# Weights loaded ahead of q and k, conversion steps at even places, and the weights' low parts made by VectorE

## The chip, the cores and the metric

The kernel runs as one program on one core of a Trainium2 chip. TensorE (PE) multiplies, VectorE (DVE), ScalarE (ACT) and GpSimd (POOL) do the elementwise work, and the queue of SyncE (SP) issues all transfers between HBM and the core's memory. The metric is device microseconds of one execution.

## What is computed

Chunked attention on 8 x 8 heads (chunks of 64 tokens), then a gated network with an RMS norm, then a second network. All is float32, on 4608 rows of 512.

```python
def _attn_ref(q, k, v):                       # 8 batches, 8 heads, 576 tokens, 64 wide; chunks of 64
    ...
    scores = scale * np.matmul(q_c, k_c.transpose(0, 1, 2, 4, 3))
    scores = scores - np.max(scores, axis=-1, keepdims=True)
    attn = np.exp(scores)
    attn = attn / (np.sum(attn, axis=-1, keepdims=True) + 1e-09)
    out = np.matmul(attn, v_c)
    ...
def _moe_ref(x, w_gate, w_val, w_out, rms_g): # 512 -> 1536 -> 512
    rms = np.sqrt(np.mean(x * x, axis=-1, keepdims=True) + 1e-06)
    xn = x / rms * rms_g
    g = xn @ w_gate
    silu = g * (1.0 / (1.0 + np.exp(-g)))
    val = xn @ w_val
    return (silu * val @ w_out).astype(np.float32)
    ...
def _moe2_ref(x, w_in, w_out):                # 512 -> 2048 -> 512
    h = x @ w_in
    relu6 = np.clip(h + 3.0, 0.0, 6.0)
    g = h * relu6 / 6.0
    return (g @ w_out).astype(np.float32)
```

## The kernel before

The rows are worked in nine blocks of 512. The first network passes over blocks 0 to 8 and leaves its result in HBM; the second passes over them again. Every number that goes into a large matmul is split into a high part in the reduced format float32r and a low part, the rest, so that a product is three matmuls (high x high, low weight x high, high weight x low).

**Weight pieces.** The weights come in pieces of 512 KB, stored as 64-bit numbers: 36 in the first network, in the order gate, val, out for each f of 0 to 11, and 32 in the second. `Prep.load` (L121) issues the load of the next piece on SP. A piece then passes four stages, two pieces (a pair) at a time: `mag` (ScalarE, L138), `bits` (VectorE, L145, L147, L149, L153, each once per piece), which makes a float32 of the 64-bit number, `hi` (ScalarE, L160), and `lo`, the low part (GpSimd, L168: piece minus high part). `Prep.step(n)` advances the pipeline by one: `lo` of the pair of three steps ago, `hi`, `bits`, and `mag` of a new pair. Raw pieces and converted ones share a pool of 36 buffers; `held` counts them, and `Prep.fill(slots, most=4)` loads while `held + 3 <= slots`, at most `most` pieces a call. The last two pieces lie in a pool of their own.

**Start.** Before block 0 the lists LOADS and START, written by hand, interleave the loads of 16 pieces, the attention of the first four groups of 128 rows, and the stages of the first pieces. After it come q, k (`load_qk`, 64 small transfers on SP, L391) and v (`load_v`, 16 transfers, L401) of pair 4. A pair is 256 rows of attention; pairs 4 and 5 are the input of block 1.

**Block 0.** For each f: gate's matmuls (`mm_up`, 12 of L542), ScalarE's sigmoid (L688), VectorE's product (L689); val's matmuls, a second product on VectorE (L694), the split of the result (ScalarE L580 for `ah`, GpSimd L581 for `al`); then the 12 matmuls of the previous f's `out` (L551 to L554). After each of these three groups stands a hook, numbered hk = 3f + o, with o = 0, 1, 2. `att_hook` does one of a pair's attention steps there, a pair in five f: o = 1 of the first f turns q and k (VectorE, L405, L406) and issues the next pair's q and k; o = 0 of the second does the scores on PE (L418), o = 1 maximum, difference and exponent; the third sum and division (L446 to L454), the fourth the transposes, the fifth the values, squares (L501) and the issue of the next v. The step `rms` of the next block stands at the first f after two pairs. `prep_hook` calls `prep_a.step(HKA[hk])` where HKA is not 0, and `fill` after it. The gate and val results have one bank of PSUM each, so gate's matmuls of f + 1 wait for the product L689 of f.

**What sets the order.** Each engine executes its instructions in program order. The program's order is that of the Python code (a manual schedule), and a wait for another engine or a transfer holds all that stands behind it on the same engine. SP waits, at each transfer, for its eighth predecessor to land, and for the buffer to be free: the q and k loads of a pair reuse the buffers that L405 and L406 of the pair before have read.

In the second network the pieces are converted in the last block of the first (HKB at its hooks) and in the first block of the second; `lo` is the same function there.

Of the kernel before, what the change touches and what calls it, by code (L numbers as in the profile page):

```python
# [36 lines left out]
    square3 mean2 spread1 norm1 spread0 root2 squares3 mean3 wl2 inv2 root3 wh3 hi1 spread2 norm0 inv3 wm5  # L37
    norm2 hi2 lo1 spread3 hi0 lo2 norm3 hi3 lo3 wh4 wm6 lo0 wl3 wb5 wb6 wh5 wl4
""".split()
HKA = [2, 0, 0, 0, 2, 2, 0, 2, 0, 0, 2, 0, 2, 0, 2, 0, 0, 2, 2, 2, 0, 0, 2, 2, 2, 2, 2, 2, 0, 0, 2, 0, 0, 2, 0, 2]  # L40
HKB = [2, 2, 2, 2, 2, 2, 0, 2, 0, 2, 2, 0, 2, 0, 2, 0, 0, 2, 2, 2, 0, 2, 0, 2, 0, 0, 2, 2, 0, 2, 2, 2, 0, 0, 0, 0]


# [1 line left out]
def fused_kernel(  # L45
# [13 lines left out]
    nc = tc.nc  # L59
# [44 lines left out]
    class Prep:  # L104
# [59 lines left out]
        def lo(self, ids):  # L164
            for i in ids:
                w = W[self.pieces[i]]
                self.held -= not self.own(i)
                nc.gpsimd.tensor_tensor(  # L168
                    w[:, 1, :], self.raw.pop(i)[:, :, 0].bitcast(F32), w[:, 0, :].bitcast(F32), op=ALU.subtract
                )  # L170

# [340 lines left out]
    def rms(blk):  # L512

        ps = PS[:, ATT, :]
        nc.tensor.matmul(ps, ones, sqs.pop(blk), start=True, stop=True)
        rt = at_p.tile([128, N], F32, tag="kT", name="rt")
        nc.scalar.activation(rt, ps, AF.Sqrt, scale=1.0 / DM, bias=eps)
        nc.vector.reciprocal(rt, rt)
        x = xf[blk]
        for c in range(KD):  # L520
            nc.vector.scalar_tensor_tensor(
                out=x[:, c, :], in0=x[:, c, :], scalar=g_sb[:, c:c + 1], in1=rt, op0=ALU.mult, op1=ALU.mult
            )
# [53 lines left out]
    def split_act(t):  # L577
        hi = ah_p.tile([128, N], F32R, tag="ah", name="ah")
        lo = al_p.tile([128, N], F32R, tag="al", name="al")
        nc.scalar.copy(hi, t)  # L580
        nc.gpsimd.tensor_tensor(lo, t, hi.bitcast(F32), op=ALU.subtract)  # L581
        return hi, lo
# [30 lines left out]
    with tc.manual_schedule():  # L613
# [3 lines left out]
        prep_a, prep_b = Prep(a_pieces), Prep(b_pieces)  # L617
# [15 lines left out]
        sqs.pop(0)  # L633
        xf.pop(0)

        nxt = Pair(N // TP)
        nxt.load_qk()
        nxt.load_v()
        state = {"att": nxt}

        def att_hook(b, hk):

            if b + 1 >= NB:
                return
            f, o = divmod(hk, 3)
            t, g = divmod(f, 5)
            a = state["att"]
            if t == N // TP:
                if hk == 3 * f + 1 and g == 0:
                    rms(b + 1)  # L650
                return
            if (g, o) == (0, 1):
                a.run("turn")
                if a.i + 1 < NPR:
                    state["nxt"] = Pair(a.i + 1)
                    state["nxt"].load_qk()
            elif (g, o) == (1, 0):
                a.run("scores")
            elif (g, o) == (1, 1):
                a.run("top", "less", "expo")  # L660
            elif (g, o) == (2, 1):
                a.run("total", "share")
            elif (g, o) == (3, 1):
                a.run("trans_p", "out_p")
            elif (g, o) == (4, 1):
                a.run("values", "out_x", "square", "squares")
                if "nxt" in state:
                    state["att"] = state.pop("nxt")
                    state["att"].load_v()

        def prep_hook(b, hk):
            if b == 0 and not prep_a.done() and HKA[hk]:
                prep_a.step(HKA[hk])
                prep_a.fill(36)
            if b == NB - 1:
                if HKB[hk]:
                    prep_b.step(HKB[hk])
                prep_b.fill(hk)

        for b in range(NB):  # L680
            prev = None
            hk = 0
            if b == NB - 1:
                load_x2(0)
            for f in range(FA):
                mm_up(GB, W["gate", f], xs)
                s = sg_p.tile([128, N], F32, tag="sg", name="sg")
                nc.scalar.activation(s, PS[:, GB, :], AF.Sigmoid)  # L688
                nc.vector.tensor_tensor(s, s, PS[:, GB, :], op=ALU.mult)  # L689
                att_hook(b, hk)  # L690
                prep_hook(b, hk)
                hk += 1
                mm_up(VB, W["val", f], xs)
                nc.vector.tensor_tensor(s, s, PS[:, VB, :], op=ALU.mult)  # L694
                a = split_act(s)
                att_hook(b, hk)
                prep_hook(b, hk)
                hk += 1
                if prev is not None:
                    mm_down_a(W["out", f - 1], prev, f == 1, False)  # L700
                att_hook(b, hk)
                prep_hook(b, hk)
                hk += 1
                prev = a
# [7 lines left out]
        for b in range(NB):  # L712
# [3 lines left out]
            for f in range(FB):  # L716
# [10 lines left out]
                a = split_act(s)  # L727
# [36 lines left out]
```

## Time and profile before

| | us |
|---|---|
| median of 3 runs | 1869.09 (1868.18 to 1870.5) |
| profiled execution | 1870.38 |
| its span, first to last instruction | 1868.6 |
| PE busy | 1782.3 (95%), 9856 matmuls |
| VectorE, ScalarE, GpSimd busy | 727.0, 601.1, 542.4 |
| first matmul of block 0 / of block 1 | 54.33 / 212.19 |
| end of the chain, by engine | PE 82%, VectorE 6%, SP's queue 3%, GpSimd 2%, transfers 2% |

Engine names in rows: PE matmul, PEld weight load, DVE VectorE, ACT ScalarE, POOL GpSimd, SPq the queue of SyncE. "a<-b" is output and input by the program's tile names: `wraw` a loaded piece, `wtmp` a scratch tile of its conversion, `w` a converted piece, `sg` the activations, `XH` and `XL` the block's input. Shares over the whole span hide that block 0 of the first network and the conversions of the second have limits of their own; rows below are therefore taken by stretch.

### The profile page before, as it was taken

The numbers are of one execution on the slowest core, as the hardware profiler recorded it, in microseconds if no ns is written. First come the engines' busy times: TensorE is split into PE (matmuls) and PEld (weight loads), VectorE is DVE, ScalarE is ACT, GpSimd is POOL, SyncE is SP. The second block draws the span as 40 slices with busy tenths as digits, with TensorE's granted clock in tenths as the row PEclk, the third lists the DMA queues.
The fourth block names the chain that finished last, engine by engine and source line by source line (L and its number), as shares of the span: only waits on it lengthen the run. The fifth ranks groups of instructions, "written<-read, shape, count | busy, mean of one in ns | idle before, by whom it ended". The sixth has DMA issues, their size and how long they took to land.

```text
span 1868.6 us, 24155 instructions
## 1 busy us (share of the span) xinstructions
PE 1782.3 (95%) x9856; PEld 1457.4 (78%) x9856; DVE 727.0 (39%) x930; ACT 601.1 (32%) x899; POOL 542.4 (29%) x395
## 2 busy tenths in 40 slices
PE   5678999999999999999999889999999999999999
PEld 4556788888888888888887678888888888888887
DVE  7787534344353534335359951121212121212121
ACT  5344423233232323233234432222323232322222
POOL 3534322112121212112125652222223232323222
PEclk8789999999999999999999999999999999999999
DMA  9362211212212121212034410110101010101000
GB/s 249 78 170 70 49 31 44 41 28 49 40 40 45 39 44 26 51 36 46 12 102 153 142 55 1 46 36 10 46 0 46 1 46 1 45 1 46 0 23 23
DMA packets 225199, 93.88 MB, mean 50 GB/s; under 512 B 192960, under 2 KB 213440, under 8 KB 223936
## 3 DMA queue, kind: packets, MB, share of 16 engines
q1 hardware_dynamic: 225088, 92.34, 18.8%
q8 instruction: 77, 1.26, 0.3%
q14 instruction: 34, 0.28, 0.1%
HBM read 73.40 MB, written 18.87 MB: 49 GB/s over the span
## 4 chain that ended last, share of the span: by engine, by line
PE 82%; DVE 6%; SPq 3%; issue 3%; POOL 2%; DMA 2%; ACT 1%; DVEq 0%; POOLq 0%; ACTq 0%
PE PS L542 45%; PE PS L563 7%; PE PS L559 7%; PE PS L560 7%; PE PS L551 4%; PE PS L552 4%; PE PS L554 4%; SPq L391 2%; POOL w L168 2%; DVE wtmp L149 1%; DVE wraw L153 1%; PE PS L418 1%; DMA wraw<-in_moe_w_gate_dram 1%; PE PS L478 1%; DVE wtmp L145 1%
## 5 line engine op out<-in xcount | busy, mean ns | idle before, releaser
L542 PE MATMUL PS<-XH,w 128*128 128x512 f32 x2880 | 729.6, 396 | 41.8 <-DVE sg L689 29.4
L581 POOL TENSOR_TENSOR al<-sg,ah 128x512 fp32r<-128x512 f32 x252 | 334.0, 1325 | 1279.9 <-ACT ah L580 1279.9
L542 PEld LDWEIGHTS PS<-XH,w 128*128 128x128 f32 x2880 | 547.5, 191 | 163.9 <-DVE sg L689 33.7
L542 PE MATMUL PS<-XL,w 128*128 128x512 f32 x1440 | 389.0, 392 | 0.0
L724 DVE SCALAR_TENSOR_TENSOR sg<-sg,PS 128x512 f32<-128x512 f32 x144 | 99.2, 689 | 623.5 <-ACT sg L723 623.5
L542 PEld LDWEIGHTS PS<-XL,w 128*128 128x128 f32 x1440 | 273.8, 190 | 57.7
L580 ACT CAST ah<-sg 128x512 fp32r<-128x512 f32 x252 | 156.3, 620 | 429.6 <-DVE sg L694 313.9
L723 ACT ACTIVATE sg<-PS,three 128x512 f32<-128x512 f32 x144 | 99.1, 688 | 445.8 <-PE PS L542 431.5
L559 PE MATMUL PS<-w,ah 128*128 128x512 f32 x576 | 224.5, 390 | 2.8 <-ACT ah L580 2.8
L560 PE MATMUL PS<-w,ah 128*128 128x512 f32 x576 | 224.1, 389 | 0.0
L689 DVE TENSOR_TENSOR sg<-sg,PS 128x512 f32<-128x512 f32 x108 | 74.0, 685 | 274.7 <-ACT sg L688 274.6
L551 PE MATMUL PS<-ah,w 128*128 128x512 f32 x432 | 175.8, 407 | 0.2 <-ACT ah L580 0.2
L552 PE MATMUL PS<-ah,w 128*128 128x512 f32 x432 | 168.5, 390 | 0.0
L563 PE MATMUL PS<-w,al 128*128 128x512 f32 x576 | 154.9, 390 | 2.1 <-POOL al L581 2.1
L688 ACT ACTIVATE sg<-PS 128x512 f32<-128x512 f32 x108 | 64.4, 596 | 246.1 <-PE PS L542 229.5
L559 PEld LDWEIGHTS PS<-w,ah 128*128 128x128 f32 x576 | 108.1, 188 | 26.4 <-ACT ah L580 4.0
L563 PEld LDWEIGHTS PS<-w,al 128*128 128x128 f32 x576 | 108.2, 188 | 25.2 <-POOL al L581 2.9
L560 PEld LDWEIGHTS PS<-w,ah 128*128 128x128 f32 x576 | 108.2, 188 | 22.4
L694 DVE TENSOR_TENSOR sg<-sg,PS 128x512 f32<-128x512 f32 x108 | 74.2, 687 | 120.5 <-PE PS L542 117.1
L554 PE MATMUL PS<-al,w 128*128 128x512 f32 x432 | 115.8, 390 | 0.1
L168 POOL TENSOR_TENSOR w<-wraw,w 128x512 fp32r<-128x512 f32 x68 | 102.0, 1525 | 17.9 <-ACT w L160 17.9
L551 PEld LDWEIGHTS PS<-ah,w 128*128 128x128 f32 x432 | 81.1, 188 | 21.4 <-ACT ah L580 2.8
(85 smaller groups left out, 1229.0 us busy)
## 6 DMA issues: line engine op xcount, KB each, us to landing
wraw<-in_moe_w_out_dram SPq DMA_DIRECT2D x28, 512.0 KB, 5.2
yd<-yst SPq DMA_DIRECT2D x18, 512.0 KB, 3.4
xf<-yd SPq DMA_DIRECT2D x9, 1024.0 KB, 6.5
wraw<-in_moe_w_in_dram SPq DMA_DIRECT2D x16, 512.0 KB, 3.9
out_dram<-ost SPq DMA_DIRECT2D x16, 512.0 KB, 3.2
wraw<-in_moe_w_gate_dram SPq DMA_DIRECT2D x12, 512.0 KB, 6.5
wraw<-in_moe_w_val_dram SPq DMA_DIRECT2D x12, 512.0 KB, 7.4
v<-in_v_dram SPq DMA_DIRECT2D x96, 64.0 KB, 2.6
```

The costliest lines, as they stand in the source:

```text
L168: nc.gpsimd.tensor_tensor(w[:, 1, :], self.raw.pop(i)[:, :, 0].bitcast(F32), w[:, 0, :].bitcast(F32), op=ALU.subtract)
L542: nc.tensor.matmul(ps, w[:, wi, c * 128:(c + 1) * 128], xs[c][xi], start=(i == 0), stop=(i == n - 1))
L551: nc.tensor.matmul(ps, wm[0], a[0], start=first, stop=False)
L552: nc.tensor.matmul(ps, wm[1], a[0], start=False, stop=False)
L554: nc.tensor.matmul(PS[:, YB + m, :], w[:, 0, m * 128:(m + 1) * 128], a[1], start=False, stop=last)
L559: nc.tensor.matmul(PS[:, YB + m, :], am, w[:, 0, :], start=first, stop=False)
L560: nc.tensor.matmul(PS[:, YB + m, :], am, w[:, 1, :], start=False, stop=False)
L563: nc.tensor.matmul(PS[:, YB + m, :], a[1][:, m * 128:(m + 1) * 128], w[:, 0, :], start=False, stop=last)
L580: nc.scalar.copy(hi, t)
L581: nc.gpsimd.tensor_tensor(lo, t, hi.bitcast(F32), op=ALU.subtract)
L723: nc.scalar.activation(s, PS[:, bank, :], AF.Relu, bias=three)
L724: nc.vector.scalar_tensor_tensor(out=s, in0=s, scalar=6.0, in1=PS[:, bank, :], op0=ALU.min, op1=ALU.mult)
```

## The change

Four things change. HKA becomes a step of two pieces at every even hook. After the start, `prep_a.fill(36, 36)` loads as many pieces as the buffers hold (16 more) ahead of q and k of pair 4, v of pair 4 is issued at hook 0, and `fill` runs at every hook of block 0 until the pieces are done. The attention steps of block 0 stand one f (three hooks) later, and so does `rms`. The low part L168 is computed by VectorE instead of GpSimd, in the start, in block 0 and in the second network's conversions.

```diff
--- before.py
+++ after.py
@@ -37,7 +37,7 @@
     square3 mean2 spread1 norm1 spread0 root2 squares3 mean3 wl2 inv2 root3 wh3 hi1 spread2 norm0 inv3 wm5
     norm2 hi2 lo1 spread3 hi0 lo2 norm3 hi3 lo3 wh4 wm6 lo0 wl3 wb5 wb6 wh5 wl4
 """.split()
-HKA = [2, 0, 0, 0, 2, 2, 0, 2, 0, 0, 2, 0, 2, 0, 2, 0, 0, 2, 2, 2, 0, 0, 2, 2, 2, 2, 2, 2, 0, 0, 2, 0, 0, 2, 0, 2]
+HKA = [0 if hk % 2 else 2 for hk in range(36)]
 HKB = [2, 2, 2, 2, 2, 2, 0, 2, 0, 2, 2, 0, 2, 0, 2, 0, 0, 2, 2, 2, 0, 2, 0, 2, 0, 0, 2, 2, 0, 2, 2, 2, 0, 0, 0, 0]
 
 
@@ -165,7 +165,7 @@
             for i in ids:
                 w = W[self.pieces[i]]
                 self.held -= not self.own(i)
-                nc.gpsimd.tensor_tensor(
+                nc.vector.tensor_tensor(
                     w[:, 1, :], self.raw.pop(i)[:, :, 0].bitcast(F32), w[:, 0, :].bitcast(F32), op=ALU.subtract
                 )
 
@@ -633,9 +633,9 @@
         sqs.pop(0)
         xf.pop(0)
 
+        prep_a.fill(36, 36)
         nxt = Pair(N // TP)
         nxt.load_qk()
-        nxt.load_v()
         state = {"att": nxt}
 
         def att_hook(b, hk):
@@ -643,10 +643,17 @@
             if b + 1 >= NB:
                 return
             f, o = divmod(hk, 3)
+            a = state["att"]
+            if b == 0:
+                if hk == 0:
+                    a.load_v()
+                    return
+                f -= 1
             t, g = divmod(f, 5)
-            a = state["att"]
+            if t < 0:
+                return
             if t == N // TP:
-                if hk == 3 * f + 1 and g == 0:
+                if o == 1 and g == 0:
                     rms(b + 1)
                 return
             if (g, o) == (0, 1):
@@ -669,8 +676,9 @@
                     state["att"].load_v()
 
         def prep_hook(b, hk):
-            if b == 0 and not prep_a.done() and HKA[hk]:
-                prep_a.step(HKA[hk])
+            if b == 0 and not prep_a.done():
+                if HKA[hk]:
+                    prep_a.step(HKA[hk])
                 prep_a.fill(36)
             if b == NB - 1:
                 if HKB[hk]:
```

On SP, behind the last load of the start, stood in the kernel before (L391 and L401 are q, k and v of pair 4, L131 weight pieces):

```order
L131 DMA wraw<-in_moe_w_gate_dram 128x4x256
L391 DMA q<-in_q_dram 32x2x32 x16
L391 DMA q<-in_q_dram 32x6x32 x16
L391 DMA k<-in_k_dram 32x2x32 x16
L391 DMA k<-in_k_dram 32x6x32 x16
L401 DMA v<-in_v_dram 64x64 x8
L401 DMA v<-in_v_dram 64x3x64 x8
L131 DMA wraw<-in_moe_w_val_dram 128x4x256
L131 DMA wraw<-in_moe_w_out_dram 128x1024
L131 DMA wraw<-in_moe_w_gate_dram 128x4x256
```

and stand in the changed kernel, after fourteen more pieces behind the last one of the start, the fifteenth and sixteenth and what follows them:

```order
L131 DMA wraw<-in_moe_w_gate_dram 128x4x256
L131 DMA wraw<-in_moe_w_val_dram 128x4x256
L391 DMA q<-in_q_dram 32x2x32 x16
L391 DMA q<-in_q_dram 32x6x32 x16
L391 DMA k<-in_k_dram 32x2x32 x16
L391 DMA k<-in_k_dram 32x6x32 x16
L401 DMA v<-in_v_dram 64x64 x8
L401 DMA v<-in_v_dram 64x3x64 x8
L391 DMA q<-in_q_dram 32x8x32 x16
L391 DMA k<-in_k_dram 32x8x32 x16
```

Sixteen pieces have moved ahead of the 64 transfers of q and k. Further down, where pair 6's q and k and the last four pieces stand, SP's order is the same in both kernels:

```order
L401 DMA v<-in_v_dram 64x4x64 x8
L391 DMA q<-in_q_dram 32x4x32 x32
L391 DMA k<-in_k_dram 32x4x32 x32
L131 DMA wraw<-in_moe_w_out_dram 128x1024
L131 DMA wraw<-in_moe_w_gate_dram 128x4x256
L131 DMA wraw<-in_moe_w_val_dram 128x4x256
L131 DMA wraw<-in_moe_w_out_dram 128x1024
```

There nothing moved on SP; the loads L391 wait for the transposes L405 and L406 of pair 5, and those stand three hooks later. On VectorE, from the products of f = 0 on, stood before (L689 and L694 are the two products of an f):

```order
L689 TENSOR_TENSOR sg<-sg,PS 128x512
L694 TENSOR_TENSOR sg<-sg,PS 128x512
L405 STREAM_TRANSPOSE qT<-q 128x1024
L406 STREAM_TRANSPOSE kT<-k 128x1024
L689 TENSOR_TENSOR sg<-sg,PS 128x512
L694 TENSOR_TENSOR sg<-sg,PS 128x512
L428 TENSOR_REDUCE mx<-PS 128x16
L438 TENSOR_TENSOR p<-PS,mx 128x2x4x64 x2
L145 TENSOR_SCALAR wtmp<-wtmp 128x512 x2
L147 TENSOR_SCALAR wtmp<-wtmp 128x512 x2
```

and now (the same two products are L697 and L702):

```order
L697 TENSOR_TENSOR sg<-sg,PS 128x512
L702 TENSOR_TENSOR sg<-sg,PS 128x512
L168 TENSOR_TENSOR w<-wraw,w 128x512 x2
L145 TENSOR_SCALAR wtmp<-wtmp 128x512 x2
L147 TENSOR_SCALAR wtmp<-wtmp 128x512 x2
L149 SCALAR_TENSOR_TENSOR wtmp<-wraw,wtmp 128x512 x2
L153 SCALAR_TENSOR_TENSOR wraw<-wraw,wtmp 128x512 x2
L697 TENSOR_TENSOR sg<-sg,PS 128x512
L702 TENSOR_TENSOR sg<-sg,PS 128x512
L405 STREAM_TRANSPOSE qT<-q 128x1024
L406 STREAM_TRANSPOSE kT<-k 128x1024
L168 TENSOR_TENSOR w<-wraw,w 128x512 x2
```

The transposes of pair 4 moved behind a conversion pair and the products of f = 1, and the low parts L168 stand among VectorE's instructions. On ScalarE, the place where the last four pieces are needed (`mag`, L138, behind the sigmoid of f = 8) stood before:

```order
L441 ACTIVATE p<-p 128x1024
L160 CAST w<-wraw 128x512 x2
L688 ACT_TABLE_LOAD
L688 ACTIVATE sg<-PS 128x512
L580 CAST ah<-sg 128x512
L160 CAST w<-wraw 128x512 x2
L688 ACTIVATE sg<-PS 128x512
L138 ACTIVATE wtmp<-wraw 128x512 x2
L580 CAST ah<-sg 128x512
```

and now:

```order
L441 ACTIVATE p<-p 128x1024
L696 ACT_TABLE_LOAD
L696 ACTIVATE sg<-PS 128x512
L138 ACTIVATE wtmp<-wraw 128x512 x2
L580 CAST ah<-sg 128x512
L138 ACTIVATE wtmp<-wraw 128x512 x2
L696 ACTIVATE sg<-PS 128x512
L580 CAST ah<-sg 128x512
```

L138 of the last pieces stands at the same place, behind the sigmoid of f = 8 and ahead of its L580; the attention step L441 in front of it moved one f nearer.

## Rows read from the trace of the kernel before

**Rows 1.** Waits on PE: 54 to 212.3 us, 215 to 930, 930 to 1160.

```profile
PE PS L542 <- DVE sg L689: 27.2, 7, 6.7
...
PE PS L418 <- DVE kT L406: 2.4, 7, 0.3
...
PE PS L542 <- DVE sg L694: 9.0, 4, 4.6
```

**Rows 2.** Timeline of VectorE in block 0 (start, us, operation, wait before it).

```profile
77.19 1.25 DVE L406 STREAM_TRANSPOSE kT<-k 128x1024 f32<-128x1024 f32 x1 [6.00 <-DMA k<-in_k_dram]
...
85.00 0.69 DVE L694 TENSOR_TENSOR sg<-sg,PS 128x512 f32<-128x512 f32 x1 [5.99 <-PE PS L542]
...
95.96 0.75 DVE L145 TENSOR_SCALAR wtmp<-wtmp 128x512 f32<-128x512 f32 x2
96.63 0.75 DVE L147 TENSOR_SCALAR wtmp<-wtmp 128x512 uint32<-128x512 uint32 x2
97.30 1.28 DVE L149 SCALAR_TENSOR_TENSOR wtmp<-wraw,wtmp 128x512 uint32<-128x512 uint32 x2
98.50 1.28 DVE L153 SCALAR_TENSOR_TENSOR wraw<-wraw,wtmp 128x512 uint32<-128x512 uint32 x2
...
115.30 0.69 DVE L689 TENSOR_TENSOR sg<-sg,PS 128x512 f32<-128x512 f32 x1 [3.62 <-ACT sg L688]
...
140.69 1.24 DVE L405 STREAM_TRANSPOSE qT<-q 128x1024 f32<-128x1024 f32 x1
...
155.38 0.68 DVE L694 TENSOR_TENSOR sg<-sg,PS 128x512 f32<-128x512 f32 x1
```

**Rows 3.** VectorE by line, 85.5 to 155.9 us (count, busy us, mean ns).

```profile
L147 DVE TENSOR_SCALAR wtmp<-wtmp 128x512 uint32<-128x512 uint32 x16 | 13.8, 901 | 0.0
L153 DVE SCALAR_TENSOR_TENSOR wraw<-wraw,wtmp 128x512 uint32<-128x512 uint32 x16 | 12.5, 819 | 0.0
L149 DVE SCALAR_TENSOR_TENSOR wtmp<-wraw,wtmp 128x512 uint32<-128x512 uint32 x16 | 12.5, 819 | 0.0
L145 DVE TENSOR_SCALAR wtmp<-wtmp 128x512 f32<-128x512 f32 x16 | 11.6, 768 | 0.0
```

**Rows 4.** Timeline of GpSimd, 86 to 92 us.

```profile
87.67 5.67 POOL L168 TENSOR_TENSOR w<-wraw,w 128x512 fp32r<-128x512 f32 x4
```

**Rows 5.** Timeline of ScalarE, 176 to 180 us.

```profile
178.94 0.67 ACT L138 ACTIVATE wtmp<-wraw 128x512 f32<-128x512 f32 x1 [8.83 <-DMA wraw<-in_moe_w_out_dram]
```

**Rows 6.** Timeline of SP's queue, 140 to 215 us.

```profile
141.96 16.28 SPq L391 DMA_DIRECT2D q<-in_q_dram  x32
158.34 15.08 SPq L391 DMA_DIRECT2D k<-in_k_dram  x32
173.60 0.35 SPq L131 DMA_DIRECT2D wraw<-in_moe_w_out_dram  x1
```

**Rows 7.** Stretches: busy of five engines, PE clock, DMA share, GB/s.

```profile
20.00:40.00 20.00, 11.18 (x180) 9.27 (x173) 18.77 (x36) 13.38 (x25) 10.25 (x10) 0.90 0.97 251
...
40.00:60.00 20.00, 11.32 (x58) 9.09 (x59) 19.57 (x41) 10.00 (x21) 15.59 (x12) 0.50 0.45 117
...
112.00:128.00 16.00, 11.96 (x100) 9.48 (x101) 12.60 (x16) 8.74 (x14) 7.96 (x5) 0.79 1.08 364
```

**Rows 8.** Chain of waits in order of time (start, us, what).

```profile
40.14 7.13 DMA wraw<-in_moe_w_gate_dram
...
75.23 1.94 DMA k<-in_k_dram
```

**Rows 9.** Line L533 over the span: ns min/median/max.

```profile
L533 DVE TENSOR_TENSOR XL<-xf,XH x34: 1359/1608/1779, 209.8 to 1775.5; 128x512 fp32r<-128x512 f32 x34
```

**Rows 10.** Timeline of PE, 211 to 214 us: block 1's first matmuls.

```profile
212.19 1.98 PE L542 MATMUL PS<-XH,w 128*128 128x512 f32 x8
```

**Rows 11.** VectorE by line, 1000 to 1097 us.

```profile
L149 DVE SCALAR_TENSOR_TENSOR wtmp<-wraw,wtmp 128x512 uint32<-128x512 uint32 x25 | 28.1, 1159 | 0.1
...
L147 DVE TENSOR_SCALAR wtmp<-wtmp 128x512 uint32<-128x512 uint32 x25 | 18.2, 764 | 0.1
```

## The prediction

> **What bounds the kernel now.** I first read who waited for whom on PE, stretch by stretch, because PE has 9856 matmuls to do in either kernel and only its gaps can change. Block 0 of the first network (54 to 212 us) holds the large gaps: matmuls of L542 waited 27.2 us there in seven places for VectorE's product L689 [rows 1]. In blocks 1 to 7 (215 to 930 us) nothing waits longer than 0.3 us at a time, and around the second network's conversions (930 to 1160) the largest item is 9.0 us behind L694 [rows 1]. So the change is worth what it does to block 0, and a little around 1000 to 1100 us.
>
> Who is late in block 0? VectorE executes in order, and L689 stands behind the weight conversions. Two things delay it. **One is GpSimd.** A pair of conversions, alone, takes 0.75 + 0.75 + 1.28 + 1.28 = 4.06 us (two instructions of each of L145, L147, L149, L153 [rows 2]). The 16 of each between 85.5 and 155.9 us took 11.6 + 13.8 + 12.5 + 12.5 = 50.4 us [rows 3]; eight pairs alone are 8 x 4.06 = 32.5. The 17.9 us too many fall beside GpSimd's low parts, such as the four L168 that run for 5.67 us from 87.67 [rows 4]. **The other is the SP queue.** VectorE waited 6.0 us at L406 for k [rows 2], and ScalarE's L138 waited 8.83 us for a weight piece, until 178.94 [rows 5]. SP issues the 64 small q and k loads of a pair one by one: the second set runs from 141.96 to the k loads' end at 158.34 + 15.08 = 173.42, so 31.46/64 = 0.49 us each, and the last four weight pieces are issued only behind them, from 173.60 [rows 6].
>
> **The change, part by part.**
>
> *Load order.* Sixteen more pieces are issued ahead of q and k of pair 4. Each piece is 0.524 MB; in 112 to 128 us, where weights dominate, the queue moved 364 GB/s [rows 7], so 1.44 us a piece. The last piece of the start lands at 40.14 + 7.13 = 47.3 us [rows 8]. By the built program an issue waits until the eighth issue before it has landed (in before the chain of waits runs over that very landing, 7.13 us [rows 8], to SP's next issue). The first q load therefore goes out when the ninth new piece lands, 47.3 + 9 x 1.44 = 60.3 us, and before the sixteenth lands at 47.3 + 16 x 1.44 = 70.3 only eight of the 64 are out. The other 56 take 56 x 0.49 = 27.4 us, to 97.7; a landing adds 1.94 [rows 8], and k is there at 99.6 us, where before it came at 77.2. The transposes L405/L406 move three hooks later, which is worth only one more conversion: In before VectorE came to L406 at 77.19 - 6.0 = 71.2 [rows 2]; one conversion pair with its low parts (some 5 us) and two products now come ahead, so it reaches L405 near 77 and stands in front of the two about 22 us, with PE behind it at the scores L418. They end at 99.6 + 1.25 = 101 us. Bounds: with no gating by the last seven pieces 60.3 + 64 x 0.49 + 1.9 + 1.3 = 95; with the pieces at the 251 GB/s of 20 to 40 us [rows 7] (2.09 us each, the last landing at 80.7) 111. I take 101, since weights alone run here as they do in 112 to 128.
>
> *Low parts on VectorE, and the even steps.* From the end of pair 4's transposes to those of pair 5 (hooks 4 to 19) VectorE has eight conversion pairs, eight pairs of low parts and the attention steps. In before the same work, to the product of hook 19, lies between 78.4 and 155.38 + 0.6 = 156.0, that is 77.6 us. From this go the wait for val's matmuls at 85.00 (6.0) and the one at 115.30 behind the late weight pieces (3.6) [rows 2], pair 5's own transposes (2.4, at 140.69 [rows 2]), one product (0.6), and of the 17.9 us beside GpSimd all but some 2 us that belong to its L581 and L454, 15.9. Sixteen low parts come in. No row shows one on VectorE alone. The nearest are L149 and L153, also 128x512 with two SBUF inputs, at 0.62 us a piece; the far one is L533, the same subtraction on VectorE, 1.36 to 1.78 us [rows 9], but always with GpSimd doing its own L533 alongside. I take 0.62: 16 x 0.62 = 9.9. Sum: 77.6 - 6.0 - 3.6 - 2.4 - 0.6 - 15.9 + 9.9 = 59.0 us; 53 if no contention is left, 71 with 1.36 for each low part. Pair 5's transposes then start at 101 + 59 = 160 us. In the start, six low parts (3.7 us) join a VectorE that is nearly full, and give back some 2.5 us of contention. That moves the first matmuls of block 0 by about 1 us, and costs nothing, because k arrives at 99.6 either way.
>
> The Trainium skill speaks on a contention that remains: SBUF — State Buffer, section "Who interferes with whom", says that a VectorE instruction with two SBUF inputs and a GpSimd one that reads SBUF exclude each other for a whole instruction. The contended rows agree with that. By it the low parts are exposed to GpSimd's L581 in their new place too, and 59 would become some 62 us if each L581 caught one; the 71 above covers it.
>
> *What follows pair 5's transposes.* The 64 loads of pair 6 may go out only when these transposes have read q and k, and the last four weight pieces still stand behind them. That queue is as long as before. ScalarE's L138 of piece 32 comes 178.94 - 140.69 = 38.3 us after L405, and block 1's first matmul at 212.19 [rows 10], 33.3 us after that. In before ScalarE needed that piece eight hooks after the transposes, and lost 8.83 us. In the new kernel it needs it at the same hook 24, but only five hooks after them: the product of hook 24 is done some 12 us after L405, and ScalarE stands about 25 us, with VectorE and PE behind it as soon as PE has used up the matmuls it may do ahead. The work behind the piece is the same; the later rms step (hook 34 for 31) and PE's lower clock after the gap (after the idle start it was granted 0.50, 1.2 GHz, in 40 to 60 us [rows 7]) I set against the gaps that PE had in the old tail too. So block 1 starts at 160 + 38.3 + 33.3 = 231.6 us: **+19.3** against 212.2. With the bounds: 95 + 53 gives +7, 111 + 71 gives +41.
>
> *Second network.* 32 low parts move to VectorE: 32 x 0.62 = 19.8 us, most of them between 1000 and 1097 us, where VectorE hardly rests. In that stretch 25 of L149 took 1159 ns in the mean and 25 of L147 764 [rows 11]; alone they take 640 and 375 (half of a pair's 1.28 and 0.75). That is 25 x 0.519 + 25 x 0.389 = 22.7 us too many; I leave a quarter to L581, so 17 are given back, against 21 low parts that GpSimd does there, 13 us. Most of the 4 us left shows on PE, which waited on VectorE there: **-3 us**. Ends: -10, if all 22.7 us go; +3, if half of the 13 us fall where nothing is given back.
>
> **Sum.** +19.3 - 3 = +16.3 us. Made against the profiled execution (1870.38 us, span 1868.6) that is 1886.7; the median of the three runs is 1.3 lower, so **1885.4 us**.
>
> **Rivals.**
> (a) *Faster: contention is what counts, the queue is hidden.* If q and k are there when VectorE reaches the transposes, only the gains stay: 15.9 - 9.9 = 6.0 from contention, 6.0 + 3.6 from the waits, 3 in the second network: 1869.1 - 18.6 = 1850.5 us. For it: those waits and the contention are real rows. Against: 64 issues of 0.49 us need 31 us, and in the new order none starts before 60.3. The Trainium skill's GPSIMD Engine Reference, section "Engine selection", would have it end here (VectorE, not GpSimd, for two-input elementwise work, about twice as fast); the rows agree on the factor, 5.67/4 = 1.42 us on GpSimd [rows 4] against 0.62.
> (b) *No change: the late pieces are hidden.* If ScalarE reaches piece 32 only when it is there, hook 19 is at 160 against 156.0, +4, less 3 in the second network: about 1870 us. For it: before, ScalarE's wait cost PE far less than 8.83 us. Against: five hooks of distance, where eight did not suffice.
> (c) *Much slower: low parts stay as dear on VectorE as L533 is.* 71 for 59 in block 0 (+12), and 21 x 0.74 = +16 in the second network: about 1913 us.
> (d) *The forecast*, slower by the queue: two waits in a row behind q and k loads.
>
> **How the numbers follow.** Forecast 0.73, (a) 0.14, (b) 0.08, (c) 0.05. This kernel's measurement can tell about 0.2%, 3.7 us, from no change. Slower 0.78 ((d) and (c)), same 0.08, faster 0.14. The forecast's own range, with most of its bounds, is 1873 to 1901; to leave out no more than 2 in 10 the range reaches down through (b): 1868 to 1901.
>
> **What would show it.** Right: VectorE idle before L405 and L406, about 20 us in all, ended by q and k near 100 us; no wait of L138 for weights from hook 2 to 18; L405 of pair 5 near 160 us; then L138 idle some 25 us until about 198; block 1's first matmul near 231; L145 and L147 near 0.4 us where GpSimd has no L581; the low part near 0.62 us. Wrong: k there before 90 us (the load rate or the wait of eight is misread), L405 of pair 5 before 146 us (contention was worth more), or L138 of piece 32 hardly waiting.

## The result, and the profile after

| | before | after |
|---|---|---|
| median, us | 1868.63 (1867.31 to 1870.5) | 1884.72 (1883.15 to 1885.23) |
| span of the profiled execution | 1868.6 | 1883.5 |
| PE busy | 1782.3 | 1778.4 |
| VectorE / GpSimd busy | 727.0 / 542.4 | 721.9 / 449.5 |
| first matmul of block 1 | 212.19 | 231.42 |
| first matmul of block 2 | 318.67 | 340.98 |

The changed kernel takes 1.0084 of the time before (95% interval 1.0066 to 1.0101): 16.1 us more, where 16.3 were forecast. The forecast was made against the profiled execution, and between the two profiled spans the difference is 14.9 us; the interval, 12.3 to 18.9 us, holds both. The work is the same, so the loss has to be gaps. Where do they stand? First the waits on PE, from 56 to 232 us (total, times, longest); this answers to the first line of [rows 1].

```profile
PE PS L418 <- DVE kT L406: 20.8, 2, 15.9
PE PS L460 <- POOL p L454: 19.2, 1, 19.2
PE PS L542 <- DVE sg L697: 9.9, 4, 5.3
PE PS L542 <- DVE sg L702: 2.5, 1, 2.5
```

Before, PE lost 27.2 us in seven places to one product. Now those are 9.9 us in four, but two single waits of 15.9 and 19.2 us have come up: for the transposes of pair 4, and for L454, which stands behind the late weight pieces (ScalarE's L138 and L580 and GpSimd's L581 come between). Both lead to SP. Its queue after the change (start, duration, what), which answers to [rows 6]:

```profile
59.46 0.37 SPq L131 DMA_DIRECT2D wraw<-in_moe_w_val_dram  x1
59.88 20.94 SPq L391 DMA_DIRECT2D q<-in_q_dram  x32
80.87 15.21 SPq L391 DMA_DIRECT2D k<-in_k_dram  x32
...
159.25 16.34 SPq L391 DMA_DIRECT2D q<-in_q_dram  x32
175.68 16.72 SPq L391 DMA_DIRECT2D k<-in_k_dram  x32
192.50 0.38 SPq L131 DMA_DIRECT2D wraw<-in_moe_w_out_dram  x1
```

The first q load of pair 4 is issued at 59.88, behind the sixteenth new piece, and the last k load at 80.87 + 15.21 = 96.08. Further down the 64 loads of pair 6 fill 159.25 to 192.40, and only then do the last four pieces go out. VectorE shows what that does (start, duration, operation, wait in brackets; answers to [rows 2]):

```profile
82.36 1.25 DVE L405 STREAM_TRANSPOSE qT<-q 128x1024 f32<-128x1024 f32 x1 [4.30 <-DMA k<-in_k_dram]
97.38 1.25 DVE L406 STREAM_TRANSPOSE kT<-k 128x1024 f32<-128x1024 f32 x1 [13.78 <-DMA k<-in_k_dram]
98.55 1.25 DVE L168 TENSOR_TENSOR w<-wraw,w 128x512 fp32r<-128x512 f32 x2
...
157.97 1.25 DVE L405 STREAM_TRANSPOSE qT<-q 128x1024 f32<-128x1024 f32 x1
...
196.96 0.43 DVE L145 TENSOR_SCALAR wtmp<-wtmp 128x512 f32<-128x512 f32 x1 [19.46 <-ACT wtmp L138]
```

There are two long idle stretches, 18.1 us in front of the transposes of pair 4 and 19.5 in front of piece 32; from the end of pair 4's transposes to the start of pair 5's are 59.4 us (98.55 to 157.97). ScalarE's wait for that piece, which answers to [rows 5]:

```profile
196.27 0.66 ACT L138 ACTIVATE wtmp<-wraw 128x512 f32<-128x512 f32 x1 [21.91 <-DMA wraw<-in_moe_w_out_dram]
```

The contention that the change was to remove is gone. VectorE by line, 98.5 to 157.9 us (count, busy us, mean ns); the same 16 of each as in [rows 3]:

```profile
L168 DVE TENSOR_TENSOR w<-wraw,w 128x512 fp32r<-128x512 f32 x16 | 11.9, 788 | 0.0
L153 DVE SCALAR_TENSOR_TENSOR wraw<-wraw,wtmp 128x512 uint32<-128x512 uint32 x16 | 10.3, 688 | 0.0
L149 DVE SCALAR_TENSOR_TENSOR wtmp<-wraw,wtmp 128x512 uint32<-128x512 uint32 x16 | 10.3, 686 | 0.0
L145 DVE TENSOR_SCALAR wtmp<-wtmp 128x512 f32<-128x512 f32 x16 | 6.1, 423 | 0.0
L147 DVE TENSOR_SCALAR wtmp<-wtmp 128x512 uint32<-128x512 uint32 x16 | 6.1, 422 | 0.0
```

The four conversion lines fell from 50.4 to 32.8 us, almost the 32.5 that eight pairs take alone, and the low parts came in with 11.9.

The start of block 1 has a gap of its own. PE, 228 to 245 us; answers to [rows 10]:

```profile
231.42 0.50 PE L542 MATMUL PS<-XH,w 128*128 128x512 f32 x1 [1.95 <-ACT XH L531]
232.09 0.49 PE L542 MATMUL PS<-XH,w 128*128 128x512 f32 x1 [0.16 <-ACT XH L531]
...
233.41 2.07 PE L542 MATMUL PS<-XH,w 128*128 128x512 f32 x5 [0.15 <-ACT XH L531]
```

PE now waits for its input, since rms stands one f later, and its clock falls. In the rows of stretches (as in [rows 7]: busy of five engines, PE clock, DMA share, GB/s), before and after:

```profile
212.00:230.00 18.00, 17.66 (x137) 14.43 (x136) 9.62 (x12) 5.56 (x8) 4.71 (x4) 1.00 0.35 91
```

```profile
231.00:249.00 18.00, 16.75 (x121) 12.70 (x122) 10.17 (x14) 7.29 (x12) 5.69 (x4) 0.91 0.28 80
```

It was granted 0.91 in the mean where before the same work ran at 1.00. The first twelve matmuls of block 1 took 5.57 us (231.42 to 236.99), where they had taken 2.72. So the delay grows from 19.2 us at block 1's first matmul to 22.3 at block 2's.

The second network gives part back. ScalarE's first cast of a block's input, L531, marks the end of each block. These two are at the end of the first network's block 7 and of the second network's block 0. Before:

```profile
954.47 2.18 ACT L531 CAST XH<-xf 128x512 fp32r<-128x512 f32 x4
...
1164.33 2.18 ACT L531 CAST XH<-xf 128x512 fp32r<-128x512 f32 x4
```

and after:

```profile
976.98 2.17 ACT L531 CAST XH<-xf 128x512 fp32r<-128x512 f32 x4
...
1179.16 2.19 ACT L531 CAST XH<-xf 128x512 fp32r<-128x512 f32 x4
```

The stretch with the second network's conversions took 209.86 us before and 202.18 after. The account by span is therefore, in us, +19.2 (to block 1) +3.1 (into block 2) +0.2 (blocks 2 to 7) -7.7 (second network's conversions), +14.8 of the 14.9 us between the two spans.

### The profile page after: what moved, and what is told of

The parts are those of the page before. It is cut to its first block, busy times and chain, and to the rows that moved or that the text cites. A ratio compares the mean times of both kernels' runs of the same rounds, so it can differ in the third digit from the quotient of the medians.

```text
span 1883.5 us, 24085 instructions
## 1 busy us (share of the span) xinstructions
PE 1778.4 (94%) x9856; PEld 1455.1 (77%) x9856; DVE 721.9 (38%) x998; ACT 600.9 (32%) x899; POOL 449.5 (24%) x327
## 4 chain that ended last, share of the span: by engine, by line
PE 83%; DVE 9%; SPq 2%; issue 2%; POOL 2%; DMA 1%; ACT 1%; DVEq 0%; POOLq 0%; ACTq 0%
PE PS L542 46%; PE PS L563 7%; PE PS L559 7%; PE PS L560 7%; PE PS L551 5%; PE PS L552 4%; PE PS L554 4%; SPq L391 2%; DVE w L168 1%; DVE wtmp L149 1%; POOL al L581 1%; DVE wraw L153 1%; DMA wraw<-in_moe_w_val_dram 1%; PE PS L418 1%; DVE wtmp L145 1%
## 5 line engine op out<-in xcount | busy, mean ns | idle before, releaser
L581 POOL TENSOR_TENSOR al<-sg,ah 128x512 fp32r<-128x512 f32 x252 | 342.5, 1359 | 1372.2 <-ACT ah L580 1372.2
L580 ACT CAST ah<-sg 128x512 fp32r<-128x512 f32 x252 | 156.3, 620 | 429.0 <-DVE sg L702 315.7
L697 DVE TENSOR_TENSOR sg<-sg,PS 128x512 f32<-128x512 f32 x108 | 74.2, 687 | 277.5 <-ACT sg L696 277.5
L702 DVE TENSOR_TENSOR sg<-sg,PS 128x512 f32<-128x512 f32 x108 | 74.3, 688 | 119.9 <-PE PS L542 116.6
L554 PEld LDWEIGHTS PS<-al,w 128*128 128x128 f32 x432 | 80.9, 188 | 19.1 <-POOL al L581 2.2
```

The lines of the kernel that those rows point to most:

```text
L554: nc.tensor.matmul(PS[:, YB + m, :], w[:, 0, m * 128:(m + 1) * 128], a[1], start=False, stop=last)
```

## The experiments

The account to be tested is the forecast's: two waits stand one after the other on VectorE's path, each behind 64 loads of 0.49 us, and the low parts on VectorE are a small gain. The rivals: VectorE was full and the low parts are the loss; or the waits cover other work, so that to remove one brings nothing.

### One part of the change at a time

**e1_low_only**: the kernel before, low parts on VectorE.

```diff
-                nc.gpsimd.tensor_tensor(
+                nc.vector.tensor_tensor(
                     w[:, 1, :], self.raw.pop(i)[:, :, 0].bitcast(F32), w[:, 0, :].bitcast(F32), op=ALU.subtract
```

> The kernel before, with the low parts L168 on VectorE and nothing else changed. Queue theory (two waits in a row behind q and k loads made the change slower, the low parts on VectorE are a gain): VectorE loses the 15.9 us of contention in block 0 and takes 9.9 us of low parts, so pair 5's transposes start some 6 us earlier than 140.69, the chain of 64 loads and four pieces moves with them, and the stretch after block 1's start gains what it gained in the changed kernel (231.42 to 1883.5 is 1652.1 us, 212.19 to 1868.6 was 1656.4: 4.3). Together about 1858 to 1859 us. Rival (VectorE was full in block 0 and the low parts on it cost): 1872 us or more.

Measured: 1859.71 us, ratio 0.9951 (0.9936 to 0.9966). The low parts are a gain, and the rival is out. The size came out right from terms that were not. By the first cast of block 1 (206.59 for 209.18 us) block 0 gave 2.6 us where 6 were expected; the first cast after the second network's conversions (1152.67 for 1164.33) is 11.7 us earlier, so these gave most of the rest (the profiled spans differ by 11.6 us, the medians by 9.0). VectorE's timeline tells why block 0 gave so little:

```profile
114.37 0.69 DVE L689 TENSOR_TENSOR sg<-sg,PS 128x512 f32<-128x512 f32 x1 [5.45 <-ACT sg L688]
...
138.90 1.24 DVE L405 STREAM_TRANSPOSE qT<-q 128x1024 f32<-128x1024 f32 x1
```

On the way to pair 5's transposes, the product that waited 3.62 us [rows 2] now waited 5.45, behind ScalarE, which stood for late weight pieces (10.00 us, until 111.72). In the old load order a faster VectorE only meets the same pieces earlier.

**e2_order_only**: the changed kernel, low parts back on GpSimd.

```diff
-                nc.vector.tensor_tensor(
+                nc.gpsimd.tensor_tensor(
                     w[:, 1, :], ...
```

> The changed kernel with the low parts L168 back on GpSimd. Queue theory: k of pair 4 is there near 97 us as in the changed kernel (97.38), VectorE then needs 59.4 - 11.9 (low parts) + 15.9 (contention back) = 63.4 us to pair 5's transposes, and the second network loses the 4.3 us again: about 1884.7 + 4.0 + 4.3 = 1893 us. Rival (the low parts on VectorE are what made the change slower): back towards 1870 us.

Measured: 1891.21 us, ratio 1.0119 (1.0104 to 1.0134). The loss stays, so it is that of the new order (loads, steps and hooks), and not of the low parts. k came at 98.52 as expected, but VectorE's stretch to pair 5's transposes was not longer:

```profile
98.52 1.25 DVE L406 STREAM_TRANSPOSE kT<-k 128x1024 f32<-128x1024 f32 x1 [13.63 <-DMA k<-in_k_dram]
...
157.59 1.24 DVE L405 STREAM_TRANSPOSE qT<-q 128x1024 f32<-128x1024 f32 x1
```

It is 157.59 - 99.7 = 57.9 us, against 59.4 with the low parts on VectorE, not 63.4. By line, 99.7 to 157.6 us:

```profile
L149 DVE SCALAR_TENSOR_TENSOR wtmp<-wraw,wtmp 128x512 uint32<-128x512 uint32 x16 | 12.5, 819 | 0.0
L145 DVE TENSOR_SCALAR wtmp<-wtmp 128x512 f32<-128x512 f32 x16 | 10.7, 710 | 0.0
L153 DVE SCALAR_TENSOR_TENSOR wraw<-wraw,wtmp 128x512 uint32<-128x512 uint32 x16 | 10.3, 683 | 0.0
L147 DVE TENSOR_SCALAR wtmp<-wtmp 128x512 uint32<-128x512 uint32 x16 | 9.3, 625 | 0.0
```

42.8 us in all: with the low parts still on GpSimd, the steps at their new places suffer 10.3 us of contention, not the 17.9 of [rows 3]. So 7.6 us of that term went with the places of the steps, whoever makes the low parts, and the 10.3 that are left are less than the 11.9 the low parts cost on VectorE.

**e8_low_a_only**: low parts on VectorE in the first network, on GpSimd in the second.

```diff
-                nc.vector.tensor_tensor(
+                (nc.vector if self.pieces is a_pieces else nc.gpsimd).tensor_tensor(
                     w[:, 1, :], ...
```

> The changed kernel with the low parts on VectorE in the first network only, on GpSimd in the second. By the positions of the blocks in the traces the second network's conversions gained 7.7 us in the changed kernel, not the 3 that the prediction gave them: about 1884.7 + 7.7 = 1892.4 us. If the prediction's term is right: 1887.7 us. Together with the run that has all low parts on GpSimd (1891.2) it tells what the low parts did in block 0: near nothing by the first figure, a gain of some 3 to 4 us by the second.

Measured: 1891.95 us, ratio 1.0126 (1.0109 to 1.0143). By the medians the second network's low parts are worth 7.2 us on VectorE, not 3; by the stretch between the casts, 207.84 us here against 202.18, they are worth 5.7. With e2 at 1891.21, those of block 0 are worth nothing in the changed order that the runs can tell.

### One load order at a time

**e3_qk_first**: q and k of pair 4 ahead of the sixteen pieces.

```diff
-        prep_a.fill(36, 36)
         nxt = Pair(N // TP)
         nxt.load_qk()
+        prep_a.fill(36, 36)
```

> The changed kernel with q and k of pair 4 issued ahead of the sixteen extra pieces, not behind them. Queue theory: k lands near 77 us, as in the kernel before (77.19). The extra pieces follow at 1.44 us each, so the pieces of hook 2 land near 80 and ScalarE's L138 waits for them some 7 us; pair 4's transposes come at 86 to 88 instead of 97.4 to 98.6, and everything behind moves with them by 10 to 13 us: about 1872 us (1868 to 1877). Rival (the wait for k is taken back later in any case, because VectorE's work is the limit): 1882 us or more.

Measured: 1870.82 us, ratio 1.0011 (1.0001 to 1.002): 13.9 us of the loss are back. ScalarE's wait for the pieces came with the size expected:

```profile
79.34 0.66 ACT L138 ACTIVATE wtmp<-wraw 128x512 f32<-128x512 f32 x1 [7.15 <-DMA wraw<-in_moe_w_val_dram]
```

Pair 4's transposes stand at 83.23 and 84.39 without a wait, pair 5's at 144.95, 13.0 us earlier than in the changed kernel. What is won at the first wait reaches the second one unabridged.

**e4_pieces_before_qk6**: pair 6's loads at hook 25, behind the last four pieces.

```diff
                     state["nxt"] = Pair(a.i + 1)
-                    state["nxt"].load_qk()
+                    if b or t == 0:
+                        state["nxt"].load_qk()
...
             elif (g, o) == (2, 1):
                 a.run("total", "share")
+                if b == 0 and t == 1:
+                    state["nxt"].load_qk()
```

> The changed kernel with the 64 loads of pair 6 issued at hook 25, behind the last four weight pieces, not at hook 19 ahead of them. Queue theory: the pieces go out when the last low parts have freed their buffers (L168 at 170.03), so L138 of piece 32 starts near 175 instead of 196.27, its wait of 21.9 us falls to 0 to 3 us, and block 1's first matmul comes near 211 instead of 231.42: about 1865 us. Rival (the late pieces are hidden, the first wait alone is the loss): 1882 us or more, with another wait in the same place.

Measured: 1862.76 us, ratio 0.9971 (0.996 to 0.9982). This removes 22.0 us with nothing else touched, and the result is faster than the kernel before. SP's queue:

```profile
162.26 0.36 SPq L131 DMA_DIRECT2D wraw<-in_moe_w_out_dram  x1
...
165.12 18.12 SPq L391 DMA_DIRECT2D q<-in_q_dram  x32
```

The pieces go out at 162.26, not 192.50, earlier than the expectation had their buffers free (170), and L138 starts at 174.79 without any wait. Pair 6's 64 loads move behind them and cost nothing, as they are needed only in block 1: L405 of pair 6, at 219.92, waits for no load.

**e5_both**: e3 and e4 together.

```diff
-        prep_a.fill(36, 36)
         nxt = Pair(N // TP)
         nxt.load_qk()
+        prep_a.fill(36, 36)
...
-                    state["nxt"].load_qk()
+                    if b or t == 0:
+                        state["nxt"].load_qk()
...
+                if b == 0 and t == 1:
+                    state["nxt"].load_qk()
```

> Both edits of the load order at once: q and k of pair 4 ahead of the sixteen extra pieces, and pair 6's 64 loads behind the last four pieces. Queue theory: the two waits stand in series on VectorE's path, so their removals add up: 1884.7 - 13.9 (q and k first alone) - 22.0 (pieces before pair 6 alone) = 1848.8 us, block 1's first matmul near 196. Rival (with one of them gone VectorE's or PE's work fills the other): no better than 1858 us.

Measured: 1849.68 us, ratio 0.9896 (0.9881 to 0.9911). Against the changed kernel 35.0 us, where the two single steps add up to 35.9. The waits are in series, and neither covered the other.

**e7_all_pieces_first**: all of the last twenty pieces ahead of q and k.

```diff
-        prep_a.fill(36, 36)
+        prep_a.fill(38, 36)
...
-                prep_a.fill(36)
+                prep_a.fill(38)
```

> The changed kernel, but filling two buffers further, so that all of the last twenty pieces stand ahead of q and k of pair 4, and none behind pair 6's loads. Queue theory: k of pair 4 comes 4 x 1.44 = 5.8 us later than 97.4, the wait of 21.9 us for piece 32 is gone and 22.0 us with it: 1884.7 + 5.8 - 22.0 = 1868.5 us. Rival (pieces further ahead cost nothing, since VectorE has slack at pair 4): 1863 us; rival (the late wait is the buffers', not the queue's): 1885 us or more.

Measured: 1871.34 us, ratio 1.0012 (1.0003 to 1.0021). The late wait vanishes here too (no L138 waits for the last pieces), so it was the queue's. The four pieces delay L406, which needs k, by 8.6 us, though, not by 5.8: it runs at 105.96 where it was 97.38. The first of them found no free buffer:

```profile
59.22 0.37 SPq L131 DMA_DIRECT2D wraw<-in_moe_w_val_dram  x1
68.46 0.34 SPq L131 DMA_DIRECT2D wraw<-in_moe_w_out_dram  x1
...
70.83 9.22 SPq L391 DMA_DIRECT2D q<-in_q_dram  x14
```

SP stood from 59.6 to 68.46 with q and k behind it, 8.8 us of that for L168 by the trace's waits; VectorE's pair of L168, which gives buffers back, ran from 67.70 to 68.98, so the first of the two ended just before the issue. 1884.72 + 8.6 - 22.0 = 1871.3: with the delay as measured, the sum fits.

### What is left in block 0

**e6_both_unshifted**: e5, with the attention steps and rms at their old hooks and pair 6's loads at hook 25.

```diff
-            if b == 0:
-                if hk == 0:
-                    a.load_v()
-                    return
-                f -= 1
+            if b == 0 and hk == 0:
+                a.load_v()
+                return
             t, g = divmod(f, 5)
-            if t < 0:
-                return
...
```

> As the kernel with both edits of the load order, and the attention steps and rms of block 0 at their old hooks (one f earlier); v of pair 4 stays behind the pieces, and pair 6's loads stand at hook 25. Queue theory: pair 4's transposes then follow k near 77 us directly instead of a conversion pair and its late pieces (83.2 us), some 6 us, and block 1's first matmuls no longer wait for their inputs L531 nor run at the low clock behind that wait (some 3 us): about 1840 us (1837 to 1845). Rival (the shift hides the wait for k, and taking it back costs a wait in front of hook 1): 1850 us or more.

Measured: 1848.46 us, ratio 0.9892 (0.9877 to 0.9906). A miss, by 8 us. The 6 us in front did not come: VectorE now stands 5.49 us for k. The second product of f = 6, which has the same place in both programs (L701 here, L705 in e5), is not earlier. This kernel:

```profile
77.36 1.25 DVE L406 STREAM_TRANSPOSE kT<-k 128x1024 f32<-128x1024 f32 x1 [5.49 <-DMA k<-in_k_dram]
...
145.28 0.68 DVE L701 TENSOR_TENSOR sg<-sg,PS 128x512 f32<-128x512 f32 x1
```

and e5:

```profile
144.59 0.67 DVE L705 TENSOR_TENSOR sg<-sg,PS 128x512 f32<-128x512 f32 x1
```

Pair 5's transposes do come 12.7 us earlier than in e5 (132.52 for 145.18), but only because they stand one f earlier in the program; that is no gain. So the rival's mechanism, a wait for k that the shift had hidden, is the one that the trace shows, though its figure is missed by 1.5 us. Block 1's first cast comes 1.7 us earlier (193.83 for 195.53). The waits on PE from 150 to 200 us name a further loss:

```profile
PE PS L542 <- DVE w L168: 4.2, 1, 4.2
```

The last low part, at hook 32, now stands behind rms on VectorE (L518 and L521, 3.35 + 2.74 us), and val's last matmuls need it.

**e9_late_steps_close**: e6, with two more conversion steps.

```diff
-HKA = [0 if hk % 2 else 2 for hk in range(36)]
+HKA = [2 if hk % 2 == 0 or hk in (27, 29) else 0 for hk in range(36)]
```

> As the kernel with both edits of the load order and the unshifted attention steps (1848.5 us), with two more conversion steps, at hooks 27 and 29. There VectorE reaches pair 5's transposes 12.7 us earlier than with the shift (132.52 for 145.18), yet block 1 starts hardly earlier, and PE waits 4.2 us for the low part L168 of the last pair, which stands behind the rms step on VectorE. If the late position of that step gave the gain back, the low part now comes at hook 29, ahead of rms, and the wait of 4.2 us goes: 1844 to 1846 us. Rival (VectorE's total work up to rms is the limit, so the steps only move the wait to a product or to rms): 1848 us or more.

Measured: 1843.53 us, ratio 0.9865 (0.9849 to 0.9882), 4.9 us less than e6. The wait for L168 is gone, and this is the best version found: 25.7 us below the kernel before. The 12.7 us that the expectation counts as given back were none: the second product of f = 6 comes at 144.76, in e5 at 144.59.

**e10_low_and_pieces**: e1, with pair 6's loads behind the last four pieces.

```diff
-                    state["nxt"].load_qk()
+                    if b or t == 0:
+                        state["nxt"].load_qk()
...
                 a.run("trans_p", "out_p")
+                if b == 0 and t == 1:
+                    state["nxt"].load_qk()
```

> The kernel before with the low parts on VectorE (1859.7 us alone) and pair 6's 64 loads behind the last four pieces; load order of the start, conversion steps and attention hooks as before. Queue theory: the pieces now go out when L168 of the pair before has freed their buffers (163.46 + some 2 us) and land near 170; L138 of piece 32 waits some 6 us, not 11.9, and VectorE starts its L145 near 171.5 where it was 176.72: about 1854.5 us. Rival (the wait is hidden here, since eight hooks lie between): 1859 us or more.

Measured: 1852.62 us, ratio 0.9913 (0.9898 to 0.9928), 7.1 us below e1. L138 of piece 32 starts at 168.01, not 176.03, and waits 3.50 us, not 11.92. The late pieces were a cost in the old order too, a smaller one: L138 stood 11.92 us for them in e1, 21.91 in the changed kernel.

**e11_both_low_gpsimd_a**: e5, with the first network's low parts on GpSimd.

```diff
-                nc.vector.tensor_tensor(
+                (nc.gpsimd if self.pieces is a_pieces else nc.vector).tensor_tensor(
                     w[:, 1, :], ...
```

> The kernel with both edits of the load order (1849.7 us), with the low parts of the first network back on GpSimd, those of the second on VectorE. It prices the low parts in block 0 where no load stands in front of anything. By the prediction's term (15.9 us of contention taken away for 9.9 us of low parts) it is 6 us slower: 1855.7 us. By the runs with the changed load order (all low parts on GpSimd 1891.2, those of the second network alone 1892.0) the low parts give nothing in block 0: 1848 to 1850 us.

Measured: 1852.0 us, ratio 0.9911 (0.9896 to 0.9925): between the two figures. Without load waits the low parts on VectorE are worth 2.3 us in block 0. VectorE's stretch from pair 4's to pair 5's transposes is 147.68 - 86.1 = 61.6 us against 145.18 - 85.8 = 59.4 in e5, a difference of 2.2 us.

No run has the even steps alone, or the later attention steps alone in the changed load order; what each of these two does by itself is not shown.

## Why the prediction was right, and where it was not

**Load order.** Right. First q load at 59.88 (60.3), k at 97.38 (99.6). VectorE stood 18.1 us (about 22). Of the terms this is the one that e3 tests by itself, and e7 gives it a second time with four pieces more. That the last pieces hold back the first q loads shows too: the 32 q loads took 20.94 us, the 32 of k behind them 15.21; the prediction had made this a little dearer than it was. The start moved block 0's first matmul by 2.6 us (56.93 for 54.33), not by about 1; this cost nothing either, as VectorE waited for k in any case.

**Work between the two waits.** The sum was right, 59.4 us (59.0), and its two large terms each missed by about 2 us in opposite ways: 17.6 us of contention went (50.4 to 32.8; 15.9 forecast), and 11.9 of low parts came (9.9). The reason given for the first was wrong in part. The prediction put the 17.9 us down to GpSimd's low parts, and rival (a) counts "15.9 - 9.9 = 6.0 from contention" as what moving them gains. Measured with the same hooks that move gains -1.5 us by stretch (e2 against the changed kernel) and +2.2 (e11 against e5). The contention was read from the old places of the steps, and 7.6 us of it was a matter of those places. Nor is it only a matter of two SBUF inputs, of which the passage that the prediction cites speaks: L145 and L147, with one, were stretched most (0.77 and 0.90 us in [rows 3] against 0.375 alone). A low part took 0.64 us when alone, near the estimate (a pair took 1.28), but one pair of the eight, at 121.29, took 2.93 us while GpSimd's L454 ran. So the total stood because the new places of the steps gave what the move of the low parts did not. The forecast had no term for that, so this agreement is luck. The lower bound of 53 does not follow from the terms either: 59.0 less the 2 us of contention that were left in is 57.

**Last pieces.** Right, and e4, e5 and e7 confirm the mechanism. From L405 of pair 5 to L138 of piece 32 were again 38.3 us (157.97 to 196.27), as from 140.69 to 178.94 [rows 2, 5]. ScalarE waited 21.91 (some 25). Beside the kernel before, the second product of f = 6, at hook 19, is only 2.0 us later (157.37 us, where it was 155.38 [rows 2]; the prediction had 160 against 156). L406 of pair 4 runs 20.2 us later (97.38 for 77.19 [rows 2]), but from there to that product it takes 18.2 us less, and 17.2 of the 19.2 us come behind it, with the last pieces.

**Behind them.** Block 1's first matmul came at 231.42 (231.6). That it agrees so closely is luck in part: pair 5's transposes came 2.0 us before the forecast, and from piece 32 to that matmul it took 35.1 us, not 33.3, a difference of the size of the wait for L531 (1.95). The step that failed is the one that set the later rms and PE's lower clock "against the gaps that PE had in the old tail too". There is a further cost of 3.1 us behind that matmul, since block 1 starts waiting for L531 and at a granted clock of 0.91, so the term for block 0 is +22.3, not +19.3. In e6, with rms at its old hook, the first eight matmuls of block 1 start without a wait and take 1.98 us, as before [rows 10].

**Second network.** Sign right, size too small: -7.7 us, not -3 (e8: 7.2 or 5.7). The terms counted contention on L149 and L147 alone. VectorE by line, 1022 to 1119 us, in the changed kernel (answers to [rows 11]):

```profile
L153 DVE SCALAR_TENSOR_TENSOR wraw<-wraw,wtmp 128x512 uint32<-128x512 uint32 x26 | 16.9, 685 | 0.1
L149 DVE SCALAR_TENSOR_TENSOR wtmp<-wraw,wtmp 128x512 uint32<-128x512 uint32 x26 | 16.9, 683 | 0.1
L145 DVE TENSOR_SCALAR wtmp<-wtmp 128x512 f32<-128x512 f32 x25 | 15.1, 640 | 0.0
L147 DVE TENSOR_SCALAR wtmp<-wtmp 128x512 uint32<-128x512 uint32 x25 | 10.5, 457 | 0.1
```

L149 fell from 1159 to 683 ns and L147 from 764 to 457 [rows 11]. L153 fell as well, from 802 to 685 ns over 26 of them, 3.0 us that were left out; L145 rose from 553 to 640 over 25, 2.2 us, also left out. Between the casts, before and after (busy of PE, PEld, VectorE, ScalarE, GpSimd):

```profile
954.47:1164.33 209.86, 193.59 (x816) 155.40 (x815) 131.66 (x176) 78.39 (x134) 99.34 (x64) 0.98 0.31 101
```

```profile
976.98:1179.16 202.18, 191.37 (x816) 154.31 (x815) 126.69 (x208) 77.97 (x133) 56.38 (x32) 0.98 0.31 104
```

VectorE's busy time fell by 5.0 us, near the 4 of the forecast. The step that missed is the one behind it, "Most of the 4 us left shows on PE": PE's gaps fell from 16.3 to 10.8 us, by 5.5, and its 816 matmuls took 2.2 us less. Why PE gains more than VectorE gives was not traced.

So the two mis-sized terms (3.0 too small a loss, 4.7 too small a gain) nearly cancel: +14.8 us by span, where 16.3 were forecast. That the median stands within 0.7 us of the forecast owes something to this and to the spread of the medians.

**The rivals.** (a) falls with its condition, a hidden queue, which does not hold in the changed order. e5, where q and k are early and the pieces not late, does come to the 1850.5 us that it gave, but by other terms: the low parts of block 0 are worth 2.3 us there and not 6.0, the second network gave more than 3, and the wait for the late pieces, which (a) left in, is gone. (b), the late pieces hidden, falls with e4: they cost 22.0 us. (c), low parts at L533's price, falls with the median of 684 ns that L168 took over all 68 in the changed kernel. That the low parts on VectorE are the loss falls with e1 and e2.

## What to carry to other kernels

A transfer queue that works in order is part of the schedule: before sixteen large loads go ahead of 64 small ones, work out when the last small one is issued and which engine stands for it, and do the same for what stands behind the small ones. Put behind each burst only what is needed last (here pair 6's loads behind the last four pieces, 22 us). And price contention at the places where the instructions will stand, not at the old ones: much of it may go, or come, with the places alone. To see what an order gains, compare two kernels at an instruction that has the same place in both, not at one that was itself moved (e6).

## What the runs showed of the hardware

With the new places of the steps, GpSimd comes to stand for VectorE in block 0. GpSimd's timeline in the changed kernel (start, duration, operation):

```profile
119.75 1.30 POOL L581 TENSOR_TENSOR al<-sg,ah 128x512 fp32r<-128x512 f32 x1 [7.97 <-ACT ah L580]
...
134.92 5.29 POOL L581 TENSOR_TENSOR al<-sg,ah 128x512 fp32r<-128x512 f32 x1 [11.25 <-ACT ah L580]
```

The same L581 takes 1.30 us when VectorE does a reduction, and 5.29 us, once in block 0, when it falls into low parts and conversions that follow each other without a break (134.04 to 139.07). Before, no L581 from 50 to 240 us took more than 1.36. Low parts on VectorE are not needed for it: in e2, with these on GpSimd, the one at 135.80 takes 4.16 us. The Trainium skill's SBUF — State Buffer, section "Who interferes with whom", says that a VectorE instruction with two SBUF inputs contends with GpSimd's reads, and that the order of issue decides who is blocked; this row agrees, with GpSimd as the one that stands, 4.0 us longer than its own 1.30. The price shows on the other engines: by the trace the next sigmoid waited 2.22 us for L581 (ScalarE, at 140.24), and VectorE's product 1.79 us for the sigmoid (at 140.87). PE has no wait for `al` in that stretch.

The same 64 conversion instructions on VectorE cost 50.4 us in the kernel before [rows 3], 42.8 in e2 and 32.8 in the changed kernel, so a mean of contended instructions belongs to one order of the code and not to the operation.
